# Squares of the first weight halves on ScalarE, of the first k and q columns on TensorE, and the first two roots tile by tile

## The chip, the cores and the metric

The kernel runs on one core of a Trainium2 chip. The metric is the device time of one execution in microseconds. A core has five engines that run side by side, each with a queue of its own that is worked off in order: PE (TensorE, matmuls), DVE (VectorE), ACT (ScalarE, activation functions), POOL (GpSimd) and SP (SyncE, which here only issues DMAs). They wait for each other by semaphores. Matmuls write to PSUM, which has eight banks here called `dense0` to `dense7`.

## What is computed

A layer norm of x (2048 tokens, 512 columns), then two branches added to x: a segment-wise attention with a memory (32 heads of 16 columns, four segments of 512 tokens) and an MLP of 1792 hidden columns with GELU.

```python
xn = _layernorm(x, axis=-1)
return x + _A_ref(xn, A_wq, A_wk, A_wv, A_wo, A_beta) + _B_ref(xn, B_w1, B_b1, B_w2, B_b2)

# _A_ref, for each segment s
logits = jnp.einsum("bhqd,bhkd->bhqk", qs, ks) * scale + mask
a_dot = jnp.einsum("bhqk,bhkd->bhqd", _softmax(logits, axis=-1), vs)
a_mem = num / den                    # phi(q) against the memory M, z of the segments before
o = g * a_mem + (1.0 - g) * a_dot    # then o @ wo

# _B_ref
y = _layernorm(x, axis=-1)
h = _gelu(jnp.einsum("bsd,df->bsf", y, w1) + b1)
return jnp.einsum("bsf,fd->bsd", h, w2) + b2
```

## The kernel before

Every large product is made of three half-precision matmuls: both factors are split into a high and a low float16 part, and high x high, high x low and low x high are added up in one PSUM bank (`split3`, L581). Before a weight can be split it is scaled by a power of two near the inverse of its size. That power comes from the sum of the squares of the weight, or of a half of it.

**Weights.** `PARTS` (L44) lists the parts in order: `qk` is the first 128 columns of k and q, `QK` their other three pieces each, `v` and `o` whole, `1a`, `1b`, `2a`, `2b` the halves of w1 and w2 (seven of 14 pieces of 128 hidden columns each, `FH`). For each part `w_load` issues the DMAs on SP, `w_square` forms column sums of squares in `am`, `w_scale` adds them over the partitions by a matmul with `ones` (L396 for k and q, L414 and L416 for the others) and makes the powers of two on DVE (L388, L392 and what follows), and `w_split` makes the high and low halves (ACT and DVE, or POOL, ACT and POOL).

There are two ways of forming the squares. On ACT, one activation `Square` with an accumulator sums the squares of each partition's columns (L353). On PE, `w_trace` (L357) multiplies every 128x128 block by itself, L382, so that the sums of squares stand on the diagonal of a PSUM tile, and DVE takes the diagonal out with the identity (L384). The blocks are read as bfloat16, the upper half of each float32. `TRACES` (L45) names the parts that go the second way: `QK`, `v`, `1a` and `2a`, that is 24, 16, 28 and 28 blocks of 128 columns. In `1a` the bias `b1` is squared on ACT as well, into column 16 of `am`.

**Norm.** For the first two pairs of 128-token tiles, `norm_sums` (L469) gets mean and variance on DVE, `norm_root` (L478) the inverse root on POOL (a sum and a power, L483 and L486, both tiles of a pair in one instruction of two columns), and `norm_apply` (L535) applies it on DVE. PE transposes the result (L564), ACT and DVE split it (L567, L568). `ratio` and `ratio_rows` make a row of factors for the MLP from the same statistics (POOL L511 to L514, PE L527, ACT L528).

**The rest.** `qk_proj` and `v_nat` project (L586), `d_job` makes the hidden layer (L586 with w1, DVE L888, ACT L895), `e_jobs` the second layer (L935), `m_job` the row maxima of the logits (PE L744, DVE L751), `s_job` the exponentials (PE L786, ACT L793), `pv` the product with the values (L820) and `out_jobs` the output (L955). L744, L786 and L684 are pairs of matmuls on 64 rows of the array each, L820 and L721 four at a time on 32 columns each; the others fill the array. Keys and queries are written to DRAM and read back in rows per head (`kd`, `qd` to `kst`, `qst`, SP queue).

**The order.** Nothing is scheduled while it runs. `streams` (L60) lists the pieces of work, in one sequence for each kind; `ORDER` (L138) is a string in which each character names the stream whose next piece is issued, and so fixes the order on every engine at once; `BANKS` (L158) gives the PSUM bank of each use. One stream, `warm`, has 24 entries `W`: a pair of matmuls of the identity by itself (L500) whose result nobody reads.

## Time and profile before

| | us |
|---|---|
| median of 3 runs (lowest, highest) | 690.71 (690.51, 691.18) |
| the profiled execution, its own time | 689.64 |
| its span in the trace | 687.9 |
| first projection on PE starts | 14.20 |
| last matmul group with the values (L820) starts | 663.07 |

The profile is one execution. Its timeline gives start and duration of each group of instructions, and in brackets the idle time of the engine before it and who ended it. A view by stages gives the busy time of each engine in a stretch, with the number of instructions, then the granted PE clock, the share of the DMA engines and GB/s. A view of waits gives who waited for whom, the sum in us, how often and the longest. Matmul durations contain the way through the array, so that neighbours overlap; the distance from start to start is what one costs in a row.

### The profile page before, as it was taken

The numbers are of one execution on the slowest core, as the hardware profiler recorded it, in microseconds if no ns is written. First come the engines' busy times: TensorE is split into PE (matmuls) and PEld (weight loads), VectorE is DVE, ScalarE is ACT, GpSimd is POOL, SyncE is SP. The second block draws the span as 40 slices with busy tenths as digits, with TensorE's granted clock in tenths as the row PEclk, the third lists the DMA queues.
The fourth block names the chain that finished last, engine by engine and source line by source line (L and its number), as shares of the span: only waits on it lengthen the run. The fifth ranks groups of instructions, "written<-read, shape, count | busy, mean of one in ns | idle before, by whom it ended". The sixth has DMA issues, their size and how long they took to land.

```text
span 687.9 us, 15912 instructions
## 1 busy us (share of the span) xinstructions
PE 680.4 (99%) x5883; PEld 393.8 (57%) x5883; DVE 502.6 (73%) x1615; ACT 472.7 (69%) x877; POOL 348.9 (51%) x574
## 2 busy tenths in 40 slices
PE   8999999999999999999999999999999999999997
PEld 6765664666554666665545555665654446475543
DVE  5899968897896668786595786977477765787522
ACT  4588998787856666678826747666956545857960
POOL 5595769664536354563652426435363325247562
PEclk9999999999999999999999999999999999999999
DMA  9788243222120441512222023330502122240001
GB/s 276 225 209 238 82 113 93 64 63 73 57 39 16 109 117 36 121 17 80 55 61 81 16 72 78 85 88 20 114 24 63 56 65 77 62 102 17 4 16 61
DMA packets 52890, 55.85 MB, mean 81 GB/s; under 512 B 4990, under 2 KB 41868, under 8 KB 52812
## 3 DMA queue, kind: packets, MB, share of 16 engines
q1 hardware_dynamic: 50508, 50.64, 26.9%
q0 software_dynamic: 2304, 4.20, 3.8%
q8 instruction: 46, 0.75, 0.5%
q14 instruction: 32, 0.26, 0.1%
HBM read 37.77 MB, written 17.05 MB: 80 GB/s over the span
## 4 chain that ended last, share of the span: by engine, by line
PE 96%; DVE 1%; DMA 1%; POOL 0%; ACT 0%; issue 0%; SPq 0%; POOLq 0%; DVEq 0%
PE dense L586 40%; PE dense L935 21%; PE dense L820 11%; PE dense L744 6%; PE dense L786 6%; PE dense L955 6%; PE dense L684 2%; PE dense L564 1%; DMA wqs<-in_A_wq_dram 1%; PE dense L700 1%; PE dense L651 1%; PE dense L382 1%; PE dense L721 1%; PE dense L757 0%; DVE xnT L568 0%
## 5 line engine op out<-in xcount | busy, mean ns | idle before, releaser
L751 DVE CUSTOM_DVE_ANT_0 dense<-dense,mask 128x384 f32<-128x384 f32 (+3 forms) x512 | 233.8, 528 | 28.5 <-PE dense L744 24.3
L793 ACT ACTIVATE pt<-dense,qkcs 128x512 f32<-128x512 f32 (+1 forms) x384 | 204.3, 628 | 45.1 <-PE dense L786 44.7
L935 PE MATMUL dense<-w2s,hT 128*128 128x512 f16 x672 | 166.7, 380 | 0.0
L586 PE MATMUL dense<-xnT,w1s 128*128 128x256 f16 x1344 | 160.0, 273 | 0.0
L807 POOL TENSOR_SCALAR_AFFINE_SELECT pt<-pt 128x256 f32<-128x256 f32 x256 | 100.3, 424 | 109.3 <-ACT pt L793 108.8
L586 PEld LDWEIGHTS <-w1s 128*128 128x128 f16 x1344 | 129.3, 98 | 29.4 <-issue 5.9
L909 POOL TENSOR_TENSOR hT<-hh,hT 128x512 f16<-128x512 f32 x64 | 67.2, 1050 | 101.4 <-ACT hT L907 89.6
L935 PEld LDWEIGHTS <-hT 128*128 128x128 f16 x672 | 60.8, 98 | 68.0 <-issue 14.0
L820 PE MATMUL dense<-pt,vt 128*32 128x512 f32 (+3 forms) x1024 | 77.2, 436 | 0.0
L751 DVE DVE_READ_ACCUMULATOR2_ANT mc<- 128x1 f32 x512 | 73.9, 144 | 0.0
L888 DVE SCALAR_TENSOR_TENSOR hT<-dense,sc,cb 128x512 f32<-128x512 f32 x64 | 43.6, 681 | 33.8 <-PE dense L586 33.5
L820 PEld LDWEIGHTS dense<-pt,vt 128*32 128x32 f32 x1024 | 31.4, 109 | 40.9 <-issue 32.4
L786 PE MATMUL dense<-qst,kst 50*128 50x384 f16 (+3 forms) x512 | 52.0, 298 | 0.0
L744 PE MATMUL dense<-kst,qst 48*128 48x384 f16 (+3 forms) x512 | 51.9, 298 | 0.0
L905 POOL TENSOR_SCALAR hh<-hT,sc 128x512 f32<-128x512 f32 x64 | 42.3, 661 | 17.5 <-ACT hT L895 11.4
L851 POOL TENSOR_TENSOR nN<-nN,oT 128x512 f32<-128x512 f32 x16 | 20.3, 1272 | 52.6 <-DVE oT L663 52.6
L907 ACT ACTIVATE hT<-hh 128x512 f16<-128x512 f32 x64 | 37.5, 585 | 13.7 <-POOL hh L905 13.7
L895 ACT ACTIVATE hT<-hT,b1t 128x256 f32<-128x256 f32 x112 | 46.5, 498 | 0.2
L955 PE MATMUL dense<-wos,oT 128*128 128x512 f16 (+2 forms) x204 | 44.0, 367 | 0.9 <-DVE acc L957 0.7
L586 PE MATMUL dense<-xnT,wks 128*128 128x512 f16 (+1 forms) x252 | 44.4, 329 | 0.0
L586 PE MATMUL dense<-xnT,wqs 128*128 128x512 f16 (+1 forms) x252 | 44.2, 328 | 0.0
L586 PE MATMUL dense<-wvs,xnT 128*128 128x512 f16 x192 | 43.6, 379 | 0.0
(229 smaller groups left out, 836.9 us busy)
## 6 DMA issues: line engine op xcount, KB each, us to landing
kst<-kd SPq DMA_DIRECT2D x32, 192.0 KB
qst<-qd SPq DMA_DIRECT2D x32, 192.0 KB
qd<-hl SPq DMA_DIRECT2D x36, 128.0 KB
kd<-hl SPq DMA_DIRECT2D x33, 128.0 KB
acc<-in_A_x_dram SPq DMA_DIRECT2D x16, 256.0 KB
acc<-in_B_b_dram POOLq DMA_DIRECT2D x16, 256.0 KB, 4.5
out_dram<-acc SPq DMA_DIRECT2D x15, 256.0 KB
xt<-in_A_x_dram SPq DMA_DIRECT2D x14, 256.0 KB
```

The costliest lines, as they stand in the source:

```text
L586: T.matmul(p, ws(k, a), xs(k, b), start=i == 0, stop=i == 3 * KT - 1)
L744: T.matmul(p[:, o:o + n], stk[i, 0][r, t, P * qb:P * qb + P], stk[i, 1][r, t, :n], start=True, stop=True)
L751: V.tensor_tensor_reduce(p[:, o:o + n], p[:, o:o + n], mask[:, 512 - n:], 1.0, -3e38, OP.add, OP.max, mc[i][:, 4 * b + t, qb:qb + 1])
L786: T.matmul(p[:, o:o + n], stk[i, 1][r, t, P * kb:P * kb + P], stk[i, 0][r, t, P * kb:], start=True, stop=True)
L793: A.activation(pt[i, 4 * b + t][:, OFF[kb]:OFF[kb] + n], p[:, c:c + n], AF.Exp, scale=qkcs[:, 1, i % NG:i % NG + 1])
L807: G.affine_select(v, v, pattern=[[0, 2], [1, P]], compare_op=OP.is_ge, fill=0.0, base=0, channel_multiplier=-1)
L820: T.matmul(p[32 * c:32 * c + 32, P * kb:], vt[s, kb][:, 4 * g + c, 16 * odd:16 * odd + 32], pt[i, 2 * c + odd][:, OFF[kb]:OFF[kb] + LEN[kb ...
L888: V.scalar_tensor_tensor(hz[:, f0:f + 1, :], p[:, :256 * n].rearrange("p (f c) -> p f c", f=n), col(CG + fh), cbt[hf].unsqueeze(1).to_broa ...
L895: A.activation(hz[:, f, :], hz[:, f, :], AF.Gelu_apprx_tanh, bias=b1t[:, fo:fo + 1])
L909: G.tensor_tensor(hT[:, z, 1, :], hht[j, c], hT[:, z, 0, :], op=OP.subtract)
L935: T.matmul(p, t[:, u, P * a:P * a + P], w2s[:, fo, v, :], start=fi == 0 and n == 0, stop=fi == FH - 1 and n == 2)
L955: T.matmul(p[:, c], o[:, u, P * b:P * b + P], wos[:, g, v, c], start=i == 0, stop=i == 3 * NG - 1)
```

## The change

Part `1a` (first half of w1) and `2a` (first half of w2) go from PE to ACT: five activations for `1a` (one for each of the four row blocks of w1, 896 columns each, and the bias) and two for `2a` (2048 and 1536 columns). Their sums are added on DVE by a `tensor_reduce` before the powers of two. Part `qk` goes the other way: the first pieces of k and q, four blocks each, are multiplied by themselves on PE and their diagonals taken on DVE. `norm_root` treats the two tiles of the first pair one after the other. `am` has three more columns. `ORDER` and `BANKS` are new tables throughout.

```diff
-TRACES = ("QK", "v", "1a", "2a")
+TRACES = ("qk", "QK", "v")
-SQUARES = {"qk": 2, "QK": 6, "v": 2, "1a": 3, "2a": 2, "1b": 4, "2b": 4, "o": 3}
+SQUARES = {"qk": 2, "QK": 6, "v": 2, "1a": 5, "2a": 2, "1b": 4, "2b": 4, "o": 3}
 ORDER = (
-    "hxahhhlhk6hkkhwxbhhlchkhdhhe6hhhfh6auhfi8$hks7hhl$8$h7%%j%8%hbhgRtc88dmr8ieRfg8fmjn&v9&9!&y&#9(nCzA)((CD++*)X9"
+    "hahshlkhhhkxbckdelhihhhf$66j6afhkhhh8k78mhh$$7hhl%x%g8h%8%bmR8&cdu8e&R8fhfhn&irt9hn9&hg&yv&9z((C)D+(A2(B*()+B("
...
-    AM = {"v": 8, "1a": 10, "1b": 12, "2a": 17, "2b": 19, "o": 23}
-    am = cst.tile([P, 28], F32, name="am")
+    AM = {"v": 8, "1a": 26, "1b": 12, "2a": 17, "2b": 19, "o": 23}
+    am = cst.tile([P, 31], F32, name="am")
...
     def w_square(m, k):
-        if m in TRACES and (m, k) != ("1a", 2):
+        if m in TRACES:
             return w_trace(m, k)
...
+        if m == "1a":
+            r, to = (flat(a)[:, 1024:1024 + 512 * FH].rearrange("p (f r c) -> p f r c", f=FH, r=KT)[:, :, k], to) if k < 4 \
+                else (b1t, am[:, 16:17])
+        elif m == "2a":
+            r = flat(a)[:, 1024 + 2048 * k:(3072, 1024 + 512 * FH)[k]]
...
+        A.activation(junk, r, AF.Square, accum_out=to)
...
     def w_trace(m, k):
-        if m == "QK":
+        if m == "qk":
             w, g = part(m, k)
+            r = piece(w, g).rearrange("p (b c) -> p b c", c=P)
+            kind, first, last, to = m + w, True, True, am[:, NG * "kq".index(w):NG * "kq".index(w) + 1]
+        elif m == "QK":
...
-        n = 4 if h else 3 if m == "o" else 1
+        n = 4 if h or m == "1a" else 3 if m == "o" else 2 if m == "2a" else 1
         p = dense()
         T.matmul(p[:, :n], ones, am[:, AM[m]:AM[m] + n], start=True, stop=True)
         if m == "1a":
-            T.matmul(p[:, 1:2], ones, am[:, 16:17], start=True, stop=True)
+            T.matmul(p[:, 4:5], ones, am[:, 16:17], start=True, stop=True)
...
-        G.tensor_scalar(a[:, 0], ag[:, :, 1], EPS, 0.0, op0=OP.add, op1=OP.add)
         nws[h] = ag, a
+        for t in (slice(0, 1), slice(1, 2)) if h == 0 else (slice(0, 2),):
+            G.tensor_scalar(a[:, 0, t], ag[:, t, 1], EPS, 0.0, op0=OP.add, op1=OP.add)
+            if h < 2:
+                G.tensor_tensor(r[:, 0, t], a[:, 0, t], mhalf[:, t], op=OP.pow)
         if h < 2:
-            G.tensor_tensor(r[:, 0], a[:, 0], mhalf[:, :2], op=OP.pow)
             return
```

What the new tables do is seen in the order of the instructions. In the changed kernel the line numbers of the functions are 10 to 12 lower. Three places follow, each before and then after.

ACT, from the evacuation of the first v projection (`vt_84`) on; `w1s` and `w2s` hold w1 and w2, `am` the sums of squares, `xnT` the transposed x, `hl` and `phq` the first k and q.

```order
L711 ACTIVATE vt_84<-dense_363 128x16x2x16
L711 ACTIVATE vt_85<-dense_409 128x16x2x16
L567 ACTIVATE xnT<-dense_423 128x4x128
L567 ACTIVATE xnT<-dense_452 128x4x128
L528 ACTIVATE cb<-dense_462 128x256
L447 ACTIVATE wqs<-wqs,qksc 128x512
L452 ACTIVATE wks<-wks 128x512
L353 ACTIVATE w1s,am<-b1t 128x14
L614 ACTIVATE hl<-dense_350 128x512
L618 ACTIVATE phk<-dense_350,qksc 128x512
L614 ACTIVATE phq<-dense_430 128x512
```

```order
L701 ACTIVATE vt_84<-dense_360 128x16x2x16
L347 ACTIVATE w1s,am<-w1s 128x896 x2
L701 ACTIVATE vt_85<-dense_395 128x16x2x16
L557 ACTIVATE xnT<-dense_418 128x4x128
L557 ACTIVATE xnT<-dense_428 128x4x128
L347 ACTIVATE w1s,am<-w1s 128x896
L435 ACTIVATE wqs<-wqs,qksc 128x512
L347 ACTIVATE w1s,am<-w1s 128x896
L347 ACTIVATE w1s,am<-b1t 128x14
L604 ACTIVATE hl<-dense_323 128x512
L608 ACTIVATE phk<-dense_323,qksc 128x512
```

Four squares of w1 stand ahead of the bias, two of them between the two v evacuations; a `cb` and a `wks` copy have gone further back, and the squares of w2 (2048 and 1536 columns) follow later among the copies of w1.

POOL, at the start, from the clear of `mhalf` on; `nw` and `stats` are the roots of the first pair, `kst`, `vt` and `mask` are cleared or filled for later.

```order
L467 MEMSET mhalf 128x4
L239 MEMSET kst_90 32x1024 x2
L229 MEMSET vt_84 128x16x16
L229 MEMSET vt_85 128x16x16
L229 MEMSET vt_86 128x16x16
L229 MEMSET vt_87 128x16x16
L239 MEMSET kst_91 32x1024 x2
L483 TENSOR_SCALAR nw<-ag 128x2
L486 TENSOR_TENSOR stats<-nw,mhalf 128x2
```

```order
L455 MEMSET mhalf 128x4
L217 MEMSET mask 128x512
L218 AFFINE_SELECT mask<-mask 128x128
L239 MEMSET kst_90 32x1024 x2
L473 TENSOR_SCALAR nw<-ag 128x1
L475 TENSOR_TENSOR stats<-nw,mhalf 128x1
L473 TENSOR_SCALAR nw<-ag 128x1
L475 TENSOR_TENSOR stats<-nw,mhalf 128x1
```

The clears of `vt` and of the second `kst` no longer stand ahead of the root, the mask does, and the root is two instructions for each tile.

SP, the loads behind v's pieces; `pt` takes the third and fourth pieces of k and q, `nN` and `nD` the second pair of x tiles, `zr` and `mhl` the gate and b1.

```order
L292 DMA pt<-in_A_wk_dram 128x4x128
L292 DMA pt<-in_A_wq_dram 128x4x128
L549 DMA nN<-in_A_x_dram 128x512
L549 DMA nD<-in_A_x_dram 128x512
L292 DMA pt<-in_A_wk_dram 128x4x128
L292 DMA pt<-in_A_wq_dram 128x4x128
L965 DMA zr<-in_A_beta_dram 128x32
L967 DMA mhl<-in_B_b_dram 14x128
L317 DMA w1s<-in_B_w_dram 128x7x128 x4
```

```order
L539 DMA nN<-in_A_x_dram 128x512
L539 DMA nD<-in_A_x_dram 128x512
L292 DMA pt<-in_A_wk_dram 128x4x128
L292 DMA pt<-in_A_wq_dram 128x4x128
L292 DMA pt<-in_A_wk_dram 128x4x128
L292 DMA pt<-in_A_wq_dram 128x4x128
L317 DMA w1s<-in_B_w_dram 128x7x128 x2
L955 DMA zr<-in_A_beta_dram 128x32
L957 DMA mhl<-in_B_b_dram 14x128
L317 DMA w1s<-in_B_w_dram 128x7x128 x2
```

The x tiles pass ahead of the third pieces of k and q, and two loads of w1 ahead of the two small ones.

## The prediction

> **What bounds the kernel now.** The page comes first: the busy shares and the chain that ended last.

> ```profile
> PE 680.4 (99%) x5883; PEld 393.8 (57%) x5883; DVE 502.6 (73%) x1615; ACT 472.7 (69%) x877; POOL 348.9 (51%) x574
> PE 96%; DVE 1%; DMA 1%; POOL 0%; ACT 0%; issue 0%; SPq 0%; POOLq 0%; DVEq 0%
> ```

> PE is busy for 99% of the span and makes up 96% of the chain. A busy PE can hide waits, so next come the waits of PE, all of them:

> ```profile
> PE dense L500 <- POOL ident masks.py:199: 1.4, 1, 1.4
> PE dense L564 <- DVE xt L535: 1.0, 1, 1.0
> PE dense L955 <- DVE acc L957: 0.7, 1, 0.7
> PE dense L414 <- DVE dense L384: 0.3, 1, 0.3
> ```

> Three of the four lie before 14.2 us, the fourth is in the last output tile. Between them PE never waits. The view by stages shows who else is near its limit:

> ```profile
> 14.20:26.00 11.80, 11.80 (x105) 8.58 (x103) 9.55 (x34) 5.88 (x12) 3.07 (x7) 1.00 1.09 308
> 26.00:36.00 10.00, 10.00 (x97) 8.03 (x96) 9.09 (x29) 6.55 (x14) 8.14 (x8) 1.00 0.50 156
> 36.00:42.40 6.40, 6.40 (x60) 5.55 (x57) 5.02 (x7) 5.56 (x10) 6.40 (x8) 1.00 1.02 219
> 42.40:59.40 17.00, 16.98 (x141) 8.86 (x140) 16.89 (x69) 15.40 (x30) 14.33 (x16) 1.00 0.87 237
> 59.40:100.00 40.60, 40.60 (x389) 24.57 (x379) 35.37 (x122) 38.03 (x72) 24.47 (x41) 1.00 0.44 115
> ```

> Columns are PE, PEld, DVE, ACT, POOL. PE is full everywhere; DVE is full too from 42.4 to 59.4 us (16.89 of 17.0), and ACT nearly so from 59.4 to 100 (38.03 of 40.6). So the time is the start of the continuous PE work, plus the sum of PE's instructions, plus a tail, as long as nothing makes PE wait anew. The timeline of PE gives the pieces:

> ```profile
> 1.43 6.18 PE L500 MATMUL dense<-ident 128*128 128x256 bf16 x32 [1.43 <-POOL ident masks.py:199]
> 12.86 0.38 PE L414 MATMUL dense<-am,ones 128*128 128x1 f32 x2 [0.32 <-DVE dense L384]
> 13.54 0.39 PE L382 MATMUL dense<-pt 128*128 128x128 bf16 x4
> 13.76 0.60 PE L500 MATMUL dense<-ident 128*128 128x256 bf16 x4
> 14.20 1.47 PE L586 MATMUL dense<-xnT,wks 128*128 128x256 f16 x12
> 24.22 1.77 PE L382 MATMUL dense<-w1s 128*128 128x128 bf16 x28
> 25.83 1.47 PE L586 MATMUL dense<-xnT,wks 128*128 128x256 f16 x12
> 31.40 1.77 PE L382 MATMUL dense<-w2s 128*128 128x128 bf16 x28
> 33.00 1.47 PE L586 MATMUL dense<-xnT,w1s 128*128 128x256 f16 x12
> 661.67 1.47 PE L935 MATMUL dense<-w2s,hT 128*128 128x512 f16 x6
> 663.07 2.36 PE L820 MATMUL dense<-pt,vt 128*32 128x512 f32 x32
> 665.36 7.30 PE L935 MATMUL dense<-w2s,hT 128*128 128x512 f16 x33
> 672.50 10.20 PE L955 MATMUL dense<-wos,oT 128*128 128x512 f16 x48
> ```

> Durations overlap, so costs are taken from start to start.

> **The change, part by part.** Traces on PE: 28 matmuls of w1 take 25.83 - 24.22 = 1.61 us, 28 of w2 33.00 - 31.40 = 1.60, or 0.057 us each. Both go. The change adds 8 traces for the first columns of k and q, but these stand before PE's first projection (14.20), where it waits anyway. From that projection on, before has 68 traces (56 and 12 for k, q), after has 16 (all for k, q, since two pieces slide behind it): 52 x 0.057 = **-2.96 us**.

> Filler: both have 24 `W` pairs (ident times ident). Four matmuls took 14.20 - 13.76 = 0.44, so a pair costs 0.22. Before has all 24 ahead of the first projection; after has 18 there, five between 15 and 24 us and one about 500 us on: 6 x 0.22 = **+1.31 us**.

> Array layouts: 33 L935 matmuls followed by a 128x128 one took (672.50 - 665.36)/33 = 0.216 each. Six followed by the 32-column L820 took 663.07 - 661.67 = 1.40, 0.10 more than 6 x 0.216. Passing between full matmuls, the 64-row pairs (L744, L786, L684) and the 32-column ones (L820, L721) costs this 0.10 each way. Counted along PE's order, there are 289 such passages before and 286 after: **-0.29 us**.

> Start of the first projection. What feeds the roots on POOL:

> ```profile
> 4.81 1.95 POOL L239 MEMSET kst<- 32x1024 f32 x2
> 6.85 0.24 POOL L483 TENSOR_SCALAR nw<-ag 128x2 f32<-128x2 f32 x1
> 7.17 0.72 POOL L486 TENSOR_TENSOR stats<-nw,mhalf 128x2 f32<-128x2 f32 x1
> 4.28 0.18 DVE L475 BATCH_NORM_AGGREGATE ag<-st 128x2 f32<-128x6 f32 x1
> 5.08 0.18 DVE L475 BATCH_NORM_AGGREGATE ag<-st 128x2 f32<-128x6 f32 x1
> 7.93 1.04 DVE L535 TENSOR_SCALAR xt<-xt,ag,stats 128x512 f32<-128x512 f32 x2 [2.67 <-POOL stats L486]
> POOL nw L483 <- DVE ag L475: 7.6, 1, 7.6
> ```

> The statistics are there at 4.46 and 5.26, but POOL clears memory until 6.76 and both roots are ready at 7.89. After, only the mask and one pair of clears stand ahead (until about 4.5). Tile by tile a root costs 0.24 + 0.72 and issue, if one column costs what two do: ready at 5.5 and 6.5, 2.4 and 1.4 us sooner. The displaced clears cost nothing: kst's second pair goes into the 7.6 us in which POOL later waits for the next statistics (last row), those of vt into the stage from 59.4 us, where POOL is busy 24.47 of 40.6. Yet the first projection hangs on something else: the scale of v (L414 at 12.86) and the weight splits after it. That chain's loads, traces and sums are the same in both, but eight further k, q traces (0.46) now stand on PE ahead of it: 13.1. Fewer fillers follow: two pairs, 0.44, after 0.25 for the sum. First projection at **13.75 instead of 14.20, -0.45 us**; bounds 13.1 (no delay) and 15.3 (below).

> Loads: nN and nD pass ahead of the third pieces of k and q, which arrive later by 2 x 256 KB at the 271 to 308 GB/s of the stages, 1.7 to 1.9 us. PE began the third piece of k at 13.54 and now comes to it at 15.05; q's at 15.5. That is close, worth 0 to 0.3.

> ScalarE now does the squares. Their prices:

> ```profile
> 8.65 0.63 ACT L353 ACTIVATE wqs<-wqs 128x512 bf16<-128x512 f32 x1 [0.18 <-DMA wqs<-in_A_wq_dram]
> 51.08 1.47 ACT L353 ACTIVATE w1s<-w1s 128x1536 bf16<-128x1536 f32 x1
> 55.65 1.04 ACT L353 ACTIVATE w1s<-w1s 128x1024 bf16<-128x1024 f32 x1
> 18.30 0.60 ACT L711 ACTIVATE vt<-dense 128x512 f32<-128x512 f32 x1 [1.70 <-PE dense L586]
> 21.84 0.60 ACT L711 ACTIVATE vt<-dense 128x512 f32<-128x512 f32 x1 [2.94 <-PE dense L586]
> ```

> 512 columns cost 0.63, 1024 1.04, 1536 1.47, about 0.42 per 512. So a square of 896 costs 0.94 (between the first two), of 1536 1.47, of 2048 about 1.90: 4 x 0.94 + 1.90 + 1.47 = 7.1 us, and 1.3 go with the k, q squares near 8 us. From 14.2 to 42.4 ACT is busy 5.88 + 6.55 + 5.56 of 28.2 us, so 10.2 are idle; two gaps of 1.70 and 2.94 are where the first two squares go. They fit, but not loosely. In ACT's order: first vt until 19.15, two squares until 21.05, the second vt and two transposed halves of x as PE delivers them until 23.4, square, a split of 0.65, square, bias 0.25: 26.2. PE: 13.75, k's half projection 1.31, traces and a filler pair 0.7, v 2.6, traces 0.45, v 2.6, so 21.4; sums, transposes and four filler pairs 2.05; two half projections 2.6: 26.05. Its w1 sum waits for the squares: 0.2. Behind that sum stand DVE's scale, POOL's product, ACT's copy and the first w1 matmul, which PE reaches at 30.45 with its pieces ready at 30.45. The 2048 square sits in ACT's queue at 29.25 to 31.15 and holds the next pieces of w1 (tile 2 wanted at 33.5, ready at 33.5; tile 6 wanted and ready near 38.8). I take **+0.3 us** in all; bounds 0 and, with squares of 896 at twice the price because they read four separate blocks' columns (no row shows that form), 3.8.

> DVE's part stays (five diagonals in both, two small sums of 0.2 more). POOL loses nothing later.

> Sum from PE: -0.45 - 2.96 + 1.31 - 0.29 + 0.3 = **-2.1 us**. What follows must move along. DVE starts the row maxima here:

> ```profile
> 42.91 0.69 DVE L751 CUSTOM_DVE_ANT_0 dense<-dense,mask 128x512 f32<-128x512 f32 x1
> 39.48 0.72 ACT L447 ACTIVATE w2s<-w2s,sc 128x512 f16<-128x512 f32 x1 [0.63 <-DVE w2s L448]
> 29.01 0.60 ACT L614 ACTIVATE phq<-dense 128x512 f16<-128x512 f32 x1 [0.50 <-PE dense L586]
> 675.17 7.53 PE dense L955 x37
> ```

> After, PE finishes w1's first seven tiles at 40.0 and DVE can begin at 41.05, 1.9 sooner; ACT's last split before the gelus moves from 39.48 to about 38.2. The stages after that keep their content, so they shift whole. The tail is a chain of DVE, ACT and POOL from the last L820 (665.36) to 675.17, and has the same members in both.

> [...]

> **Rivals.** [...]

> B, *hidden anyway*: the row maxima need qst and kst, written and reread through DRAM. If those arrive as late as before, or DVE's full stage begins no sooner than 42.9, PE's 2.1 us go into a new wait near 40 us, and only the passages stay: -0.3, 690.4. Against it: phq, the last head of that path, is written at about 28.1 instead of 29.01, its low half on DVE sooner too, since no w1 or w2 diagonal stands ahead of it there, and PE showed no wait at the row maxima.

> C, *ScalarE becomes the bound*, slower: a square of 896 at double price adds 0.94 four times, 3.8 us, in a queue whose order leaves nothing spare before the w1 sum. PE waits there, and DVE, POOL and the gelus stand in line behind; the full DVE stage and an ACT that is 94% busy from 59.4 to 100 us make nothing good. The sum without the 0.3 is -2.4; with 3.8 of waits it is +1.4, 692.1. From 3.8 us of new waits on it is slower, whichever form of square is the dear one. For it: the tight places above. Against it: ACT's 10.2 idle us in that stretch, of which the squares need 7.1.

> **How the numbers follow.** The profiled execution took 689.64 with a span of 687.9; the median of the three runs is 690.71, and the gain is taken off that: 690.71 - 2.1 = 688.6. A measurement of this kernel tells about 0.2%, 1.4 us, from no change. Forecast (687.2 to 689.3) 0.66, A 0.12, B 0.12, C 0.10. Without the +0.3, and with the 13.1 bound, the sum is -3.1, so the low end is 687.3. Both same-side rivals end below 690.9, which is the high end; C is left out. Faster 0.65, same 0.25, slower 0.10.

> **What would show it.** Right: first projection near 13.75; no L382 matmul from 24 us on (their line number moves); PE waits of under 0.5 us in sum between 14 and 660; DVE's row maxima from about 41; the last L820 ending near 663.3. [...] B: a PE wait at the first row maxima. C: 128x896 squares of well over 0.94 us, and PE waiting for ACT at the two sums. The prediction is wrong in its basis if PE has waits spread over the 100 to 660 us stretch, where only the order of the work differs: there I took the new order to be as tight as the old one.

## The result, and the profile after

| | before | after |
|---|---|---|
| median of 5 runs (lowest, highest) | 690.71 (690.51, 691.81) | 696.09 (695.61, 698.89) |
| the profiled execution, its own time | 689.64 | 695.86 |
| its span | 687.9 | 694.2 |

The ratio is 1.0070, with a 95% interval of 1.0043 to 1.0096: slower by 3.0 to 6.6 us. The prediction had 687.2 to 689.3 for its forecast and 690.9 as the high end with its rivals; both are missed. The page of the profile after, busy shares and chain:

```profile
PE 680.8 (98%) x5835; PEld 390.3 (56%) x5835; DVE 507.5 (73%) x1617; ACT 478.5 (69%) x885; POOL 350.2 (50%) x576
PE 91%; DVE 4%; ACT 2%; DMA 1%; issue 1%; POOL 0%; SPq 0%; POOLq 0%; DVEq 0%; ACTq 0%
```

PE's 680.8 is no smaller than before, with 48 matmuls fewer. The chain now has 4% of DVE and 2% of ACT, so PE waits somewhere in the middle. From the view of PE's waits (sum, times, longest):

```profile
PE dense L576 <- DVE hT L878: 2.6, 1, 2.6
...
PE dense L747 <- DVE mc L741: 0.9, 1, 0.9
...
PE dense L776 <- ACT pt L783: 0.6, 1, 0.6
```

Before had four waits. The three rows here are new and lie behind 40 us. Three more new ones, of 0.19 to 0.51 us, are waits for loads at 7.3, 8.5 and 9.4 us (L370), ahead of the first projection. PE's timeline gives the offset between the two executions, here after's rows and then before's at the first row maxima and the first full-width key projection:

```profile
14.44 1.47 PE L576 MATMUL dense<-xnT,wks 128*128 128x256 f16 x12
40.98 1.19 PE L734 MATMUL dense<-kst,qst 48*128 48x512 f16 x8
45.37 4.44 PE L576 MATMUL dense<-xnT,wks 128*128 128x512 f16 x12 [2.61 <-DVE hT L878]
84.66 2.76 PE L576 MATMUL dense<-xnT,wks 128*128 128x512 f16 x12
678.74 10.18 PE L945 MATMUL dense<-wos,oT 128*128 128x512 f16 x48
```

```profile
42.41 0.82 PE L744 MATMUL dense<-kst,qst 48*128 48x512 f16 x8
79.76 2.76 PE L586 MATMUL dense<-xnT,wks 128*128 128x512 f16 x12
```

At the row maxima the changed kernel is 1.43 us **ahead**. At 84.66 it is 4.90 behind, and at the last output block 6.24 (678.74 against 672.50). So 6.3 us go between 41 and 85, and 1.3 more in the rest. The largest wait starts with DVE and POOL. Their timelines after:

```profile
37.76 0.75 DVE L436 SCALAR_TENSOR_TENSOR w2s<-w2s,sc 128x512 f16<-128x512 f32 x1 [0.56 <-ACT w2s L435]
39.02 1.51 DVE L878 SCALAR_TENSOR_TENSOR hT<-dense,sc,cb 128x512 f32<-128x512 f32 x2
40.45 4.47 DVE L436 SCALAR_TENSOR_TENSOR w2s<-w2s,sc 128x512 f16<-128x512 f32 x1
44.84 0.47 DVE L878 SCALAR_TENSOR_TENSOR hT<-dense,sc,cb 128x256 f32<-128x256 f32 x1
45.24 0.68 DVE L741 CUSTOM_DVE_ANT_0 dense<-dense,mask 128x512 f32<-128x512 f32 x1
```

```profile
39.51 0.69 POOL L438 TENSOR_SCALAR w2s<-w2s,sc 128x512 f32<-128x512 f32 x1
40.14 1.06 POOL L907 DMA_DIRECT2D acc<-in_B_b_dram  x1
40.94 1.46 POOL L442 TENSOR_TENSOR wks<-wks 128x512 f16<-128x512 f32 x1
42.09 0.97 POOL L895 TENSOR_SCALAR hh<-hT,sc 128x512 f32<-128x512 f32 x1
42.76 0.96 POOL L438 TENSOR_SCALAR w2s<-w2s,sc 128x512 f32<-128x512 f32 x1
43.43 0.94 POOL L438 TENSOR_SCALAR pt<-pt,qksc 128x512 f32<-128x512 f32 x1
47.07 1.15 POOL L899 TENSOR_TENSOR hT<-hh,hT 128x512 f16<-128x512 f32 x1 [2.70 <-ACT hT L897]
```

The same instruction, DVE's split of w2 (its low half, both operands in SBUF), took 0.75 at 37.76 and **4.47** at 40.45. It ended at 44.92, 0.55 us after POOL's unbroken run (44.37); four of POOL's instructions began while it stood there. Behind it stood the eviction L878 that frees PE's bank (44.84; with a split of 0.75 it would have been 41.2) and the row maxima (45.24). The windows show what PE did after its wait (columns PE, PEld, DVE, ACT, POOL, then the granted clock, DMA share, GB/s):

```profile
44.00:46.00 2.00, 0.63 (x2) 0.24 (x2) 2.00 (x5) 0.65 (x2) 0.37 (x1) 0.89 0.93 202
46.00:48.00 2.00, 2.00 (x6) 0.76 (x5) 2.00 (x9) 1.98 (x4) 0.93 (x1) 0.50 0.40 132
```

The granted clock, 1.00 from 40 to 44, falls to 0.50, and eight matmuls of 512 columns stand 0.427 us apart instead of 0.216. The wait costs twice.

### The profile page after: what moved, and what is told of

Same layout as the page of the kernel before. It is cut to its first block, busy times and chain, and to the rows that moved or that the text cites. A ratio compares the mean times of both kernels' runs of the same rounds, so it can differ in the third digit from the quotient of the medians.

```text
span 694.2 us, 15846 instructions
## 1 busy us (share of the span) xinstructions
PE 680.8 (98%) x5835; PEld 390.3 (56%) x5835; DVE 507.5 (73%) x1617; ACT 478.5 (69%) x885; POOL 350.2 (50%) x576
## 4 chain that ended last, share of the span: by engine, by line
PE 91%; DVE 4%; ACT 2%; DMA 1%; issue 1%; POOL 0%; SPq 0%; POOLq 0%; DVEq 0%; ACTq 0%
PE dense L576 37%; PE dense L925 21%; PE dense L810 10%; PE dense L776 6%; PE dense L945 6%; PE dense L734 6%; PE dense L674 2%; DVE dense L741 1%; PE dense L554 1%; DMA wqs<-in_A_wq_dram 1%; PE dense L690 1%; PE dense L641 1%; DVE w2s L436 1%; PE dense L711 0%; ACT w2s L347 0%
## 5 line engine op out<-in xcount | busy, mean ns | idle before, releaser
L878 DVE SCALAR_TENSOR_TENSOR hT<-dense,sc,cb 128x512 f32<-128x512 f32 x64 | 43.6, 681 | 36.6 <-PE dense L576 35.1
L895 POOL TENSOR_SCALAR hh<-hT,sc 128x512 f32<-128x512 f32 x64 | 43.9, 685 | 20.2 <-ACT hT L885 11.2
L576 PE MATMUL dense<-xnT,wks 128*128 128x512 f16 (+1 forms) x252 | 46.1, 337 | 2.6 <-DVE hT L878 2.6
```

The source lines that it names most:

```text
L576: T.matmul(p, ws(k, a), xs(k, b), start=i == 0, stop=i == 3 * KT - 1)
L895: G.tensor_scalar(hht[j, c], hz[:, z, :], col(SHH + j % 2), 0.0, op0=OP.mult, op1=OP.add)
```

## The experiments

Terms used below. The **shut-out** is that split of 4.47 us. The **head** is the order up to the 220th step (about 66 us), the **tail** what follows. Ratios stand against the kernel before on the same chip, with a 95% interval.

### Three ways to take the shut-out away, and the squares alone

Theory: POOL holds DVE's two-operand split off, and that is where the time goes. Rivals: the time goes with the new order as a whole, or with ScalarE's squares.

Split issued later, behind the second row-maximum job:

```diff
-            V.scalar_tensor_tensor(l, r, s, h, op0=OP.mult, op1=OP.subtract)
+            low = lambda: V.scalar_tensor_tensor(l, r, s, h, op0=OP.mult, op1=OP.subtract)
+            if (m, n) == ("2a", 3):
+                late[0, 1] = low
+            else:
+                low()
...
+        if (i, j) in late:
+            late.pop((i, j))()
```

> The changed kernel, with the low half of w2's row tile 3 (VectorE, the scalar_tensor_tensor that took 4.47 us at 40.45) issued on VectorE behind the second row-maxima job; ScalarE's and GpSimd's orders untouched. Theory (that instruction was shut out by GpSimd's unbroken run 39.51 to 44.37 and held up VectorE's queue): the eviction of the last hidden tile ends by 41.5 instead of 45.31, TensorE's wait of 2.61 us at 42.5 falls under 0.3, the key projection behind it runs at 0.216 a matmul from its start (12 in about 2.6 us instead of 4.37), the first row maximum starts by 41.8; the time falls by 4.5 to 6 to about 690.6 (689.8 to 691.6). Rival squares (ScalarE loaded with the squares is what holds the stage): the wait moves to ScalarE's GELU and the time stays above 694.5. Rival order (the new order loses its time later, at 100 to 660 us): under 1 us gained, 695 or more.

POOL's subtraction for wks (the `#`) moved four steps back, behind the scaling of the first GELU piece, so that POOL waits in between:

```diff
-    "*o)CXX!joX(+*,,D)XX*,X-3,#XFYZ,F9091FPy...
+    "*o)CXX!joX(+*,,D)XX*,X-3,XFYZ#,F9091FPy...
```

> The changed kernel, with GpSimd's subtraction for wks (1.46 us at 40.94) put behind its scaling of the first GELU piece, so that GpSimd has to wait for ScalarE in the middle of its run; VectorE's order is untouched. Theory: the split at 40.45 gets in where GpSimd waits and takes at most 1.7 us instead of 4.47; TensorE's wait of 2.61 falls under 0.8; the time falls by 3.5 to 6, to 690 to 692.5, less if the key projection now waits for the later wks. Rival squares or rival order: the split may become short, but the time stays above 694.5.

Order as it is, but the split's first operand is a PSUM bank instead of w2 (the low half of that piece is then not w2's):

```diff
-            V.scalar_tensor_tensor(l, r, s, h, op0=OP.mult, op1=OP.subtract)
+            u, s = (dp[0], col(CG)) if (m, n) == ("2a", 3) else (r, s)
+            V.scalar_tensor_tensor(l, u, s, h, op0=OP.mult, op1=OP.subtract)
```

> The changed kernel, with nothing moved; the one VectorE split at 40.45 takes its first operand from the PSUM bank of the hidden tile evicted just before, and that eviction's scale, in place of w2's row tile in SBUF (the low half of that tile is left out). Theory in its narrow form (two operands read from SBUF beside GpSimd are what shuts VectorE out): the instruction takes 0.7 to 0.9 us in the same place, with GpSimd busy all along, and the time falls to about 690.6 (689.8 to 691.6). If VectorE is shut out for another reason (its write to SBUF, a semaphore, the order of its queue): it stays at 4 us or more and the time at 695 to 697.

The kernel before with only the squares of the w1 and w2 halves moved to ScalarE:

```diff
-TRACES = ("QK", "v", "1a", "2a")
+TRACES = ("QK", "v")
...
+                r = flat(a)[:, 1024:1024 + 512 * FH].rearrange("p (f q c) -> p f q c", f=FH, q=2)[:, :, k]
...
+                r = flat(a)[:, 1024 + 2048 * k:(3072, 1024 + 512 * FH)[k]]
```

> The kernel before, in its own order, with only the first halves of w1 and w2 summed by squares on ScalarE (two squares each: 1792 and 1792, 2048 and 1536 columns) instead of 56 diagonal matmuls on TensorE and two diagonal sums on VectorE. By the prediction's own terms: 56 matmuls go, about 3 us of TensorE's path, and 6.7 us of ScalarE come on in 18 to 36 us; without a collision 688 to 690.5. If the squares are what costs (rival squares): 692 or more, with TensorE waiting there for ScalarE. If a VectorE split is then shut out by GpSimd in this order too, it shows as one of over 2 us, with a wait of TensorE behind it.

| | median us (runs) | ratio |
|---|---|---|
| split later | 694.77 (6) | 1.0054 [1.0035, 1.0072] |
| POOL pauses | 694.27 (5) | 1.0043 [1.0027, 1.0060] |
| PSUM operand | 695.14 (4) | 1.0057 [1.0035, 1.0080] |
| squares alone | 699.98 (4) | 1.0125 [1.0110, 1.0140] |

Each of the three removed the shut-out. DVE's timeline, in the kernel in which POOL pauses and in that with the PSUM operand:

```profile
40.48 0.74 DVE L436 SCALAR_TENSOR_TENSOR w2s<-w2s,sc 128x512 f16<-128x512 f32 x1
```

```profile
39.36 0.74 DVE L437 SCALAR_TENSOR_TENSOR w2s<-dense,sc,w2s 128x512 f16<-128x512 f32 x1
```

In the second POOL still ran its unbroken run, and the split stood at the same place as in after, 0.31 us behind the start of POOL's DMA. With one operand in PSUM the split took 0.74 beside that run, with both in SBUF 4.47: so it is the two SBUF operands on DVE, against POOL, that make the 4.47. In after the split is recorded as starting (40.45) 0.49 us ahead of POOL's L442 (40.94), yet it stood behind that one and three more.

The gain, though, was 0.9 to 1.8 us against after's 696.09, not the whole loss: the theory that all of it sits there fell. (Where POOL pauses, three of the five executions had a mean granted clock of 0.994 to 0.997, and the other two took 692.72 and 693.75. The first of these is the profiled one: behind a lead of 1.4 us at the row maxima PE waits 0.7, 1.0, 0.9 and 0.6, which makes 1.8 of loss, against the 1.7 by which it stands above the median of the kernel before.) In the profiled execution of the PSUM run 3.5 us came back in a new place, since an earlier head asks for the last pieces of w1 before they are loaded (PE's waits, then ACT's timeline; `rc` holds one such piece):

```profile
PE dense L402 <- ACT w1s L347: 3.5, 1, 3.5
```

```profile
60.03 0.63 ACT L347 ACTIVATE w1s<-rc 128x512 bf16<-128x512 f32 x1 [3.74 <-DMA rc<-in_B_w_dram]
```

The squares alone, in the old order, cost 9 us. PE's waits there:

```profile
PE dense L423 <- ACT w2s L362: 2.9, 1, 2.9
PE dense L423 <- ACT w1s L362: 1.7, 1, 1.7
```

The granted clock fell behind these waits as well (0.72 on average from 30 to 36 us, 0.50 from 42 to 44). The squares themselves are not dear there: 1.70 us for 1792 columns, 1.90 for 2048. They stand too late in ACT's queue. So the waits that rival C of the prediction described exist in the old order, for another reason than a double price. In after no such wait stands at either sum, and the squares have the predicted prices.

### Head and tail apart

The order was cut at the 220th step and the pieces crossed; the second takes the head in which POOL pauses, the third the head as it is.

```diff
-ORDER = (the order of the changed kernel)
+ORDER = (the head of one order) + (the steps of the other that the head has not issued, in their order)
```

> The kernel before up to about 66 us (its first 221 steps, its squares, its roots), then the order of the changed kernel, with the banks that its own table gives. Rival order (the new order of the work behind 66 us is less tight): the small waits of TensorE that the changed kernel shows there, 0.94 at 83, 1.12 at 197 and some 1.6 in pieces between 300 and 640, come back, and the time rises by 2.5 to 3.7, to 693.5 to 694.7. Theory alone (all that is lost is lost at 40 to 50 us): 690.4 to 691.4, no change.

> The changed kernel up to about 66 us, with GpSimd's subtraction for wks moved behind its first GELU piece as in the run before (so without the shut-out split), then the order of the kernel before. Theory and rival order together: at 70 us this head was 0.4 ahead of the kernel before, and the old order keeps that: 690.0 to 691.0, with no TensorE wait over 0.3 between 80 and 660 us. Theory alone: the tail makes no difference, 693.5 to 694.5 as in the run before.

> The changed kernel up to about 66 us with nothing in it altered, so with the shut-out split, then the order of the kernel before. With the two runs before (new order throughout, with and without the shut-out split: 696.1 and 694.3; shut-out removed and old order behind 66 us: 690.6) it fills the fourth place. If the two losses add: the split lasts over 4 us again, TensorE's wait of about 2.6 us is there again, 692.3 to 693.5. If the shut-out costs nothing in the end (the full VectorE stage behind it would have held TensorE anyway): 690.2 to 691.2.

| | median us (runs) | ratio |
|---|---|---|
| old head, new tail | 692.38 (11) | 1.0013 [1.0004, 1.0022] |
| new head without shut-out, old tail | 690.64 (12) | 0.9996 [0.9981, 1.0011] |
| new head as it is, old tail | 696.32 (12) | 1.0061 [1.0039, 1.0083] |

The new tail alone costs 692.38 - 691.22 (the median before, on that chip) = 1.2 us, or 0.9 (0.3 to 1.5) by the ratio; 2.5 to 3.7 had been expected. Among its PE waits, which neither the kernel before nor the second kernel here has:

```profile
PE dense L757 <- DVE mc L751: 0.9, 1, 0.9
PE dense L786 <- ACT pt L793: 0.6, 1, 0.6
```

They are the rows 0.9 and 0.6 of after. The new head without the shut-out is not measurably slower than before, nor faster. The third result is too dear for the shut-out alone. Its twelve executions had mean granted clocks of 0.992 to 0.997, and the windows of the profiled one (columns as above), the only one that has them, show where the clock fell:

```profile
4.00:8.00 4.00, 2.46 (x17) 1.64 (x16) 2.70 (x7) 0.60 (x1) 3.34 (x8) 1.00 0.93 264
10.00:12.00 2.00, 1.98 (x11) 1.51 (x10) 1.07 (x9) 0.38 (x1) 0.21 (x1) 0.50 1.04 368
```

PE is busy 2.46 of the 4 us from 4 to 8, and at 10 the granted clock is 0.50. With PE this slow in the head, the price of the shut-out can't be read from this kernel. Of the executions with a new head, no early filler and no shut-out, 14 of 41 had a mean clock below 0.9975 (without the PSUM run, whose clock falls behind its wait of 3.5); of the kernel before 13 of 134. In the second kernel the four such executions have a median of 693.34, the eight others 690.37: about 3 us.

### What makes DVE wait for five instructions

POOL issues a DMA inside the run (L907, 1.06 us). Behind it each POOL instruction is recorded 0.28 us longer than its like ahead of it (L438 0.96 against 0.69), as if begun before the last one had ended. Theory: with the DMA ahead POOL never lets go between instructions. Rival: any unbroken run of POOL does it. First, the DMA taken out of the run in after:

```diff
-    "*o)CXX!joX(+*,,D)XX*,X-3,#XFYZ,F9091FPyFz.Z9,FRF40/1-R!FZFp04.
+    "*o)CXX!joX(+*,,D)XX*,X-,,#XFYZF9091FPyFz.Z9,FRF40/1-R!F3ZFp04.
```

> The changed kernel, with GpSimd's DMA (b2 added to acc) taken out of the run that begins at 39.5 and put behind the sixth row-maxima job, and its scaling of w2's row tile 4 drawn ahead into that place, so that GpSimd still runs without a pause from 39.5 to about 43.3; VectorE's order is untouched. If the DMA ahead of it is what lets GpSimd shut VectorE out instruction after instruction (behind it GpSimd's instructions were recorded 0.28 longer, each begun before the one ahead had ended): the split at 40.45 gets its turn after one GpSimd instruction and takes 0.75 to 1.7 us; 692 to 694. If any unbroken run shuts it out: it lasts until about 43.3, 2.8 us, with a TensorE wait of about 1 us behind it; 694 to 696.

Then the kernel before, with its DMA one step later:

```diff
-    ",(X3)*,X,9.XoXX
+    ",(X)*3,X,9.XoXX
```

> The kernel before, with the same GpSimd DMA (at 38.13) put behind the one GpSimd instruction that follows it (at 38.94), nothing else touched. It then stands right where VectorE issues the split of w2's row tile 3 (40.24), and GpSimd's run behind it has no pause until 47. If the DMA causes the shut-out: that split takes over 3 us, TensorE waits behind the hidden tiles' evictions, and the time rises by 2 to 7, to 692.5 to 697.5. If not: it takes 0.75 to 1.6 and the time stays within 1 us of the kernel before.

The same, and the split's DVE part behind an eviction of the hidden layer, so that it meets the run; and that split with the DMA in its old place:

```diff
+            if (m, n) == ("2a", 3):
+                late[0, 5] = low
...
+        if (j, f) in late:
+            late.pop((j, f))()
```

> The kernel before, with GpSimd's DMA put behind the next GpSimd instruction, and the low half of w2's row tile 3 issued on VectorE one eviction later (behind that of hidden tiles 4 and 5), so that it now comes behind the DMA, inside GpSimd's run. If the DMA lets GpSimd shut VectorE out: the split takes over 2 us, up to GpSimd's next pause, the last eviction of the hidden tiles and the row maxima come as much later, and the time rises by 1.5 to 6 to 692 to 697. If an unbroken run with a DMA ahead is not enough: under 1.7 us, and 690 to 692.

> The same as the run before, but with GpSimd's DMA left in its old place: only the split of w2's row tile 3 is issued one eviction later on VectorE, inside GpSimd's run from 40.4 to 47.6, which has no DMA close ahead. If it takes the DMA to shut VectorE out: the split gets its turn after one GpSimd instruction, 0.75 to 1.7 us, and the time stays within 1 us of the kernel before. If any unbroken run does: over 3 us here too, 693 or more.

And the head with the DMA out of the run before the old tail:

> The changed kernel up to about 66 us with GpSimd's DMA put later (as in the run of that name), then the order of the kernel before: the form with none of the losses found so far but the third split inside VectorE's full stage (0.67) and a late GpSimd product for w2 (0.5 to 0.7 of TensorE). At 42 us the new head was 1.4 ahead of the kernel before. Expected 689.5 to 691.0; under 690.0 would beat the kernel before, 690.5 or more says that the stage of the row maxima takes back all that the new head gains.

| | median us (runs) | ratio | the split |
|---|---|---|---|
| DMA out of the run, after | 694.28 (6) | 1.0043 [1.0028, 1.0058] | 0.95 |
| DMA later, before | 690.59 (10) | 0.9995 [0.9982, 1.0008] | not met |
| DMA later, split later, before | 695.05 (10) | 1.0049 [1.0025, 1.0073] | 4.40 |
| split later alone, before | 691.68 (10) | 0.9996 [0.9973, 1.0019] | 1.55 |
| DMA out of the run, old tail | 693.43 (12) | 1.0019 [0.9998, 1.0041] | 0.95 |

The second missed its aim: the split began at 42.38, a tenth before the DMA at 42.49, and so met nothing. The third and fourth are the clean pair, here in the kernel **before**; their orders differ in the place of that DMA alone. DVE and then POOL, first with the DMA right ahead of the split:

```profile
41.96 4.40 DVE L450 SCALAR_TENSOR_TENSOR w2s<-w2s,sc 128x512 f16<-128x512 f32 x1
```

```profile
40.44 1.07 POOL L925 DMA_DIRECT2D acc<-in_B_b_dram  x1
41.26 1.00 POOL L456 TENSOR_SCALAR w2s<-w2s,sc 128x512 f32<-128x512 f32 x1
...
44.39 1.42 POOL L460 TENSOR_TENSOR wks<-pt,wks 128x512 f16<-128x512 f32 x1
```

and with the DMA in its old place, at 38.52, so that 3.7 us and four POOL instructions lie between it and the start of the split:

```profile
42.26 1.55 DVE L450 SCALAR_TENSOR_TENSOR w2s<-w2s,sc 128x512 f16<-128x512 f32 x1
```

```profile
42.11 1.15 POOL L460 TENSOR_TENSOR w2s<-w2s 128x512 f16<-128x512 f32 x1
43.25 1.13 POOL L913 TENSOR_SCALAR hh<-hT,sc 128x512 f32<-128x512 f32 x1
```

POOL runs unbroken in both. With the DMA close ahead the split waits for the whole run; otherwise for one instruction, and then POOL's next one waits for DVE (L913 at 1.13 instead of 0.69). This shows the place of the DMA as the trigger. The price between these two is 695.05 - 691.68 = 3.4 us.

A DMA ahead is not enough by itself, though. The kernel before has the same DMA and two splits close behind it, the first of which begins ahead of POOL's next instruction as in after. POOL, then DVE:

```profile
38.13 1.05 POOL L917 DMA_DIRECT2D acc<-in_B_b_dram  x1
38.94 1.46 POOL L454 TENSOR_TENSOR w1s<-w1s 128x512 f16<-128x512 f32 x1
40.39 1.16 POOL L450 TENSOR_SCALAR w2s<-w2s,sc 128x512 f32<-128x512 f32 x1
```

```profile
38.65 0.74 DVE L448 SCALAR_TENSOR_TENSOR w2s<-w2s,sc 128x512 f16<-128x512 f32 x1
40.24 0.75 DVE L448 SCALAR_TENSOR_TENSOR w2s<-w2s,sc 128x512 f16<-128x512 f32 x1 [0.19 <-ACT w2s L447]
```

Neither is held up. Here only the one instruction behind the DMA is longer, and the next begins when it has ended, without the overlap; the kernel with the split later alone has the same rhythm. In the shut-outs the overlap lasts through the whole run. What decides between the two was not tried.

The first and fifth kernels lost part of their gain to PE waiting for the late loads of w1, 1.5 and 1.4 us, and in the profiled executions of both the clock fell in the head. The fifth had been expected at 689.5 to 691.0.

### The filler

Theory: the new head loses because fewer fillers stand in PE's early waits. From the head in which POOL pauses with the old tail, the five `h` (a filler pair each) that came later were put back early, without and with the shut-out:

```diff
-    "hahshlkhhhkxbckdelhihhhhf$66j6afhk
+    "hahshlkhhhkxbckdelhihhhhhf$h6h6hj6afhk
```

> The changed kernel up to about 66 us, without the shut-out split (GpSimd's subtraction for wks behind its first GELU piece) and with the old order behind 66 us, as in the second run of that kind (690.64); in addition the five filler pairs that the change had put between 15 and 24 us go back into TensorE's first waits (two ahead of the first transposes, one behind each of the first three traces). If the missing fillers are why the granted clock fell to 0.5 near 8 to 15 us in some executions of the new head: it stays at 1.00 there in the profile, and the mean clock is 0.998 or more in nearly all runs. Five pairs of 0.22 leave TensorE's path, 1.1 us: 689.5 (689.0 to 690.3), faster than the kernel before by 1 to 2. If the clock has another cause: a third of the runs below 0.9975, 690 to 692.

> The same kernel as the run before, but with GpSimd's subtraction for wks in the changed kernel's place, so that VectorE's split is shut out again. The price of the shut-out by itself, with the head's clock out of the way: TensorE waits 2.6 to 3.2, its clock may fall after that (another 1.8), and the full VectorE stage begins 2 to 4 later: 3 to 4.5 slower than the run before, 692.5 to 694.5. If the old order hides it: within 1 us of the run before.

Then the last pair, which the new order has near 64 us, early too, with the old tail and with the new one:

> The run with early filler (690.50), with the last filler pair too (it had come to stand at 64 us, where TensorE waited 0.6 for its bank) put ahead of the first transposes; nothing left out. That wait of 0.9 in all goes: 689.4 to 690.0, faster than both kernels by 0.1 to 0.2%. If a wait behind it (the maxima, w1's last pieces) takes its place: 690.3 to 690.7.

> The same head as the run before (all filler early, split not shut out), but behind 66 us the changed kernel's own order. The price of the new order by itself, with the head's clock out of the way: its small waits were 2.3 in the profile of three kernels; 1.5 to 3 slower than the run before, 691.3 to 692.8. If the new order costs nothing: within 0.5 of it.

| | median us (runs) | ratio |
|---|---|---|
| five pairs early | 690.50 (11) | 0.9995 [0.9986, 1.0004] |
| the same with the shut-out | 694.07 (6) | 1.0053 [1.0037, 1.0068] |
| all pairs early, old tail | 692.50 (12) | 1.0017 [1.0005, 1.0029] |
| all pairs early, new tail | 692.57 (12) | 1.0017 [0.9999, 1.0034] |

With the early fillers 4 of 47 executions of such kernels without the shut-out had the low clock (the last kernel of the next section left aside, whose clock falls behind a wait of 3.0), against 14 of 41. But the early fillers ran on other chips, and there the kernel before had it less often too (3 of 56 against 10 of 78), so the counts alone don't show the fillers as the cause. The profiled executions add to it: the clock fell in the head in four of all twenty, with PE busy for 1.94, 2.37, 2.46 and 2.59 us of the 4 from 4 to 8 us; one of these is the kernel before with its DMA later. Two others had 2.40 and 2.58 and kept it, and so did all fourteen from 2.72 on. The early fillers give 3.50 to 4.00. The same window in the first kernel (columns as above), where the clock stayed at 1.00 behind it:

```profile
4.00:8.00 4.00, 4.00 (x27) 3.14 (x25) 2.25 (x6) 0.41 (x1) 3.41 (x9) 1.00 1.03 302
```

The first two rows of the table share a chip and a head with a steady clock: the **shut-out costs 694.07 - 690.50 = 3.6 us**. PE is 1.63 us ahead at the row maxima in the first, yet the kernel ends where the kernel before does (689.5 had been expected). The third, with the last pair moved, is 2 us slower than the first, on another chip. The move changes the bank table behind it, and in its profiled execution PE's waits have a new one at the row maxima:

```profile
PE dense L734 <- DVE mc L741: 2.1, 1, 2.1
```

The third and the fourth differ in the tail alone, ran on one chip and come out alike, where 1.5 to 3 us had been expected. By this pair the new tail costs nothing; but the third has that wait of 2.1 and the fourth has not, it waits 0.9 and 0.6 like after. Against the first kernel the new tail in the fourth costs 1.0017 - 0.9995, or 1.5 us, over two chips and with the last pair moved as well. So the price of the tail is known only as 0.9 to 1.5 us, and it depends on the head.

### Two that ruled something out

The row-max stage has three splits on DVE in after and two in before. The third left out (the low half of one piece of q or k is cleared by GpSimd instead, so that it is missing from the product):

```diff
+            if (m, n) == ("QK", 3):
+                G.memset(l, 0.0)
+            else:
+                V.scalar_tensor_tensor(l, r, s, h, op0=OP.mult, op1=OP.subtract)
```

> The run with early filler (690.50), with the one VectorE split that the change moved into the stage of the row maxima (low half of wq's third piece) left out and that half cleared by GpSimd. If the stage of the row maxima, full on VectorE, is what takes back the new head's gain: it lasts 0.7 to 1.1 less than 17.7, TensorE's transpose of the maxima comes as much sooner, and the time falls by 0.5 to 1.1 to 689.4 to 690.0. If TensorE's wait for wks at 41.5 (0.7, with 1.07 in all) is what takes it back: 690.3 to 690.7.

And an attempt to keep the head's lead, from the kernel with five pairs early: wks earlier, the DMA well behind.

```diff
-    "*o)CXX!joX(+*,,D)XX*,X-3,XFYZ#,F9091FPyFz.Z9,FRF40/1-R!FZFp04.
+    "*o)CXX!joX(+*,,D)XX*#,X-,XFYZ,F9091FPyFz.Z9,FRF40/1-R!FZ3Fp04.
```

> The run with early filler, nothing left out: GpSimd's subtraction for wks is put ahead of its scaling of w2's row tile 2 (at 39.5), and its DMA behind the scaling of the third GELU piece, where GpSimd then idles. No DMA ahead of the split, so by the shut-out's rule the split takes 0.75 to 1.0; wks is ready at 40.7, so TensorE's wait of 0.7 at 41.5 goes. If that wait counts: 689.3 to 690.0, faster than both kernels. If the full VectorE stage behind it decides: 690.2 to 690.7, as without it.

The first came to 690.75 (12), 1.0009 [0.9995, 1.0022]. The stage lasted 17.7 us with or without that split (DVE idled 1.2 instead), so the split is not what costs. (Its profiled execution is one of three above 693 us, of the twelve: PE waits 2.8 for a late piece of w1 near 63 us.) The second came to 695.65 (6), 1.0076 [1.0064, 1.0089], although PE was 2.6 ahead at the row maxima, more than in any other kernel here. Its PE waits, and ACT's timeline there beside that of the kernel before:

```profile
PE dense L402 <- ACT w1s L347: 3.2, 2, 3.0
```

```profile
59.94 0.63 ACT L347 ACTIVATE w1s<-rc 128x512 bf16<-128x512 f32 x1 [3.27 <-DMA rc<-in_B_w_dram]
```

```profile
57.14 0.63 ACT L353 ACTIVATE w1s<-rc 128x512 bf16<-128x512 f32 x1 [0.35 <-DMA rc<-in_B_w_dram]
```

A head that is 2.6 us earlier asks for a piece of w1 that comes 2.8 us **later** than before. The wait of 3.0 at 62 us is followed by the half clock again. ACT got that piece 9.4 us after the load's issue instead of 4.9; why was not tried.

## Why the prediction was wrong

**The start: right in kind, 0.7 short.** The roots of the first tiles end at 5.76 and 6.77 (forecast 5.5 and 6.5). The first projection starts at 14.44, forecast 13.75: three waits of 0.19 to 0.51 us for loads (L370) stand ahead of it. In the profile of the kernel with all pairs early and the new tail, which has none of them, it starts at 13.73. The sum for v in between starts at 13.76, forecast 13.1; the rows gave 12.86 + 0.46 = 13.32, so 13.1 was too early by itself.

**The sum over PE's work: right up to the row maxima.** No trace stands behind 20 us, and at the row maxima PE is 1.43 us ahead, 0.7 less than forecast for the same reason (42.41 to 40.98). (One slip in the range: 690.71 - 3.1 is 687.6, not the 687.3 of its low end.)

**The squares: right.** They took 0.94, 1.90 and 1.47 us, and reading four separate blocks costs nothing extra. ACT's timeline after:

```profile
19.70 0.94 ACT L347 ACTIVATE w1s<-w1s 128x896 bf16<-128x896 f32 x1
29.79 1.90 ACT L347 ACTIVATE w2s<-w2s 128x2048 bf16<-128x2048 f32 x1
32.82 1.47 ACT L347 ACTIVATE w2s<-w2s 128x1536 bf16<-128x1536 f32 x1
```

Rival C therefore did not occur. That the kernel got slower, as C alone had it, is no point in its favour: neither of its signs, dear squares and waits at the two sums, is there. **B** (a wait at the first row maxima for qst and kst) did not occur either. **A**: no run shows the 15.3 us that bounds the start of the first projection from above, nor the term on which A has its 0.12 among the chances. In their place the runs show 14.44 in after, whose clock read 1.00 up to there, and 16.34 in the kernel before with its DMA later, whose clock read 0.50 from 12 to 14 us. With the new head the clock fell to 0.50 between 8 and 16 us in three profiled executions, and the executions of the second crossed kernel with a low mean clock took 3 us longer (693.34 against 690.37).

**The step that failed first** is "DVE's part stays ... POOL loses nothing later", and with it "The stages after that keep their content, so they shift whole". They do not keep their neighbours. Work was counted by engine, and no price was put on DVE and POOL standing side by side in a new combination: that term stood at nothing. The new order put a DVE split into a POOL run behind a DMA, where it took 4.47 us instead of 0.75 and PE waited 2.61; in the two pairs that isolate it, this costs 3.4 and 3.6 us with the half clock behind it. The trace of before had shown the small form of it, POOL and DVE:

```profile
26.28 1.16 POOL L454 TENSOR_TENSOR wks<-wks 128x512 f16<-128x512 f32 x1 [1.35 <-ACT wks L452]
```

```profile
26.41 1.58 DVE L448 SCALAR_TENSOR_TENSOR wqs<-wqs,qksc 128x512 f16<-128x512 f32 x1
```

A split that takes 0.75 elsewhere took 1.58 where POOL had begun 0.13 earlier. The prediction gave that row no price.

**The second** is "I took the new order to be as tight as the old one", which the prediction itself had named as its weak basis. The new tail costs 0.9 to 1.2 us by the crossed kernel and 1.5 by one other comparison; with a third, on one head and one chip, nothing.

**The third** is a price that was not in the sum: the granted clock behind a wait of PE. In the prediction's view by stages it reads 1.00 from 14.2 to 100 us in before, and the same was taken for after. After does not keep it: behind the wait of 2.61 us it reads 0.50 from 46 to 48. How long a wait has to be for that was not shown: 2.61 us was enough here, and behind 2.99 in the third crossed kernel the clock stayed at 1.00.

**What became of the gain.** Without the shut-out, with the old tail and the early fillers, PE's 1.6 us of lead at 42 us end in 690.50 against 690.93. The lead goes in the stage of the row maxima: DVE works at them from 42.91 to 59.16 us before, and from 41.30 to 59.00 in that kernel, so 1.6 us at the start are 0.2 at the end. Two short waits in its profile (0.7 for wks, which stands later in that kernel, and 0.6 near 65 us) make 1.3 of it; that they are what takes the lead back is argued and not shown, since the kernels without one or the other wait at new places. No kernel of the study holds its lead. Where the head was made earlier still, PE waited for the last pieces of w1. Together: shut-out 3.4 to 3.6, tail 0.9 to 1.5, head 0.0 to -0.4, which gives 3.9 to 5.1; measured 5.4 by the medians, 3.0 to 6.6 by the interval. What is left lies within the interval, but the parts do not simply add. By them, after without the shut-out should stand 0.5 to 1.5 us above the kernel before, and its four such kernels stood 3.1 to 4.2 above it. Late loads of w1 (1.5 and 3.5) and a low clock are part of that; the rest is open, and that the sum comes near the measured loss is in part luck. No version beat the kernel before by more than a measurement can tell.

## What to carry to other kernels

When a change reorders work, counting what each engine has to do is not enough: look at every long DVE instruction with two SBUF operands and see which POOL instructions now stand beside it, above all behind a DMA that POOL issues (4.47 and 4.40 us here instead of 0.75). An earlier start is worth only as much as the next loads, and the slack of the first full engine, let it keep (here 1.6 us at 42 us were 0.2 at 59). A filler that looks idle may hold the clock (likely here, not proved: it fell in four of six profiled executions in which PE was busy for 1.94 to 2.59 of the 4 us from 4 to 8, and in none of fourteen from 2.72 on): before moving it, read how full PE is in the first microseconds.
